# Blocked attention and a gated FFN on one core: 17 units written out in single steps, pair sums folded together, narrow weight loads placed behind short products

## The chip, the cores and the metric

The kernel runs on one core of a Trainium2 chip. Five engines take part: TensorE (PE, with its weight loads shown apart as PEld), VectorE (DVE), ScalarE (ACT), GpSimd (POOL) and SyncE (SP), which issues the transfers. The metric is the device time of one execution in microseconds. Three runs of the kernel before took 1071.14 to 1071.73 us, median 1071.46.

## The reference

Eight batches and eight heads of attention over 576 tokens with 64 features. The mask is by blocks of 64 tokens: a query sees its own block and all before it. The heads are joined to 512 features, and 4608 tokens go through an FFN of 2048 with silu.

```python
scores = scale * np.matmul(q, k.transpose(0, 1, 3, 2))
scores = np.where(block_i >= block_j, scores, -1000000000.0)
scores = scores - np.max(scores, axis=-1, keepdims=True)
attn = np.exp(scores)
attn = attn / (np.sum(attn, axis=-1, keepdims=True) + 1e-09)
x = np.matmul(attn, v)                       # then [8*576, 512]
h = x @ w_in
out = (h * (1.0 / (1.0 + np.exp(-h)))) @ w_out
```

q, k and v are float32. The FFN weights come as float64.

## The kernel before

**Precision.** A float32 operand is split in two parts that TensorE takes at its fast rate: a high part (a cast on ScalarE) and a low part (a subtraction on GpSimd or VectorE). A product is the sum of high by high, high by low and low by high. The weights' float64 is taken apart by words: ScalarE rebiases (`rebias`, L155), VectorE puts the bits together in three operations (`bits`, L159), then come `hi` and `lo`. There are 32 such pieces of weights, w0 to w31; each has a staging buffer that it shares with later work.

**The attention of the first 128 tokens of each batch** is done apart: groups a and b (block 0, class `First`, L427) and c0 to c3 (block 1, class `Second`, L486). They give the first four token blocks of the FFN.

**Units.** The 448 later queries of one batch and head are a unit (class `Unit`, L209), u0 to u63. Keys stand on partitions. The scores come in five segments (`SEG`, L38) of 448, 320, 192, 448 and 64 columns, in three PSUM banks; each segment is two products (`scores`, L242), with q's high and low part. VectorE takes the maximum (`max`, `max2`), subtracts it (`sub`), ScalarE takes the exponential and casts the high part (`exp`, `p_hi`), GpSimd makes the low part (`p_lo`). Nine products with the values (`pv`, L326) sum into bank U: the weights are 128 columns, the values' high part in one half and their low part in the other, and the moving operand is p's high part (ph) or low part (pl). VectorE adds p over the keys (`sums`, then `sums2`, L312, which folds 32-row strips by `quad_fold`, L196, for each unit); `lower` and `fold` join the halves of U, and once two units (a pair) are done `finish` normalizes and splits them into FFN input.

**FFN.** 18 blocks of 256 tokens, 8 steps each. A step has two chunks of 12 products of 256 columns (`ffn1`, L541), a silu on ScalarE, a split of g, and two chunks of 6 products of 512 columns (`ffn2`, L566): 576 chunks in all. In the text a chunk is one `ffn`.

**Order.** The schedule is by hand: every engine takes its instructions in the order in which they are recorded. The table `ORDER` (L47) writes out the weights, the early groups and the first units, up to 72 chunks; a chunk is the word `ffn`, silu and split are `silu` and `part`. From unit 2 on a loop (L661) records each unit the same way, with its predecessors' later stages between, and with `pace` chunks for each: a count that reaches 152 chunks at unit 17, and 7 a unit after that. When the units are used up, the rest of the FFN follows. Forty small products on zeros (`WARM`) stand at the head of TensorE's queue.

Of the kernel before, what the change touches and what calls it, by code (L numbers as in the profile page):

```python
# [47 lines left out]
a.load w0.load w1.load b.load a.load_v a.scores b.scores w2.load a.max:0 w3.load a.max:1 w0.rebias a.sub:0 a.exp:0 a.sub:1  # L48
w0.bits:0 w1.rebias a.sum:0 w0.bits:1 a.exp:1 w4.load a.sum:1 a.norm:0 w0.bits:2 a.norm:1 a.turn:1 w1.bits:0 w0.hi a.turn:0
w1.bits:1 w0.lo b.max:0 a.back:1 w1.bits:2 a.back:0 b.max:1 b.sub:0 a.pv b.load_v a.hi:0 b.sub:1 w5.load a.hi:1 w1.hi w1.lo  # L50
w2.rebias b.exp:1 w4.rebias a.lo:0 a.lo:1 w2.bits:0 b.sum:1 w5.rebias b.exp:0 ffn w2.bits:1 ffn b.sum:0 w2.bits:2 b.norm:0
w3.rebias b.norm:1 w6.load w3.bits:0 b.turn:0 w3.bits:1 w3.bits:2 silu b.turn:1 w2.hi w4.bits:0 b.back:0 b.back:1 w3.hi b.pv
c0.load w7.load w4.bits:1 w2.lo w3.lo b.hi:0 w4.bits:2 b.lo:0 ffn c0.scores:0 w6.rebias b.hi:1 w5.bits:0 part w4.hi w5.bits:1
w8.load b.lo:1 w5.bits:2 w5.hi c0.max:0 w6.bits:0 ffn silu c0.sub:0 ffn w6.bits:1 w4.lo w9.load w5.lo c0.exp:0 w6.bits:2 c0.sum:0
w10.load ffn w8.rebias w7.rebias c0.norm:0 w7.bits:0 w7.bits:1 ffn w9.rebias c0.turn:0 part c0.back:0 c0.scores:1 c0.load_v
w7.bits:2 w6.hi w8.bits:0 w7.hi c0.max:1 w11.load c0.sub:1 w8.bits:1 w6.lo w10.rebias w8.bits:2 w7.lo c0.exp:1 w12.load c0.sum:1
w8.hi c0.norm:1 silu ffn ffn w9.bits:0 w9.bits:1 w9.bits:2 ffn w10.bits:0 c1.load c0.turn:1 c0.back:1 w11.rebias c0.pv w8.lo w9.hi
w10.bits:1 c0.hi w9.lo w10.bits:2 part w10.hi w12.rebias c0.lo w13.load w11.bits:0 ffn ffn w10.lo w11.bits:1 c1.load_v silu
c1.scores:0 w14.load w11.bits:2 part w13.rebias c1.max:0 c1.sub:0 w12.bits:0 w11.hi w11.lo c1.exp:0 ffn ffn ffn silu w12.bits:1
w15.load w12.bits:2 w16.load c1.sum:0 ffn w14.rebias c1.norm:0 w13.bits:0 w13.bits:1 part w13.bits:2 c1.turn:0 c1.back:0  # L60
w14.bits:0 ffn c1.scores:1 c2.load c1.max:1 w12.hi w12.lo w13.hi w13.lo ffn c1.sub:1 w15.rebias c1.exp:1 w17.load silu ffn ffn
w14.bits:1 w14.bits:2 ffn c1.sum:1 c1.norm:1 w15.bits:0 w15.bits:1 w14.hi w14.lo c1.turn:1 c1.back:1 w15.bits:2 w16.rebias part
ffn w15.hi w16.bits:0 c1.pv w17.rebias w16.bits:1 w18.load w16.bits:2 ffn w16.hi c1.hi w19.load w17.bits:0 w15.lo w17.bits:1 ffn
c1.lo c2.scores:0 w18.rebias w17.bits:2 w16.lo c2.max:0 w17.hi c2.sub:0 w18.bits:0 w17.lo silu w20.load w19.rebias ffn ffn
c2.load_v w18.bits:1 ffn w21.load w18.bits:2 ffn part c2.exp:0 w18.hi c2.sum:0 w22.load c2.norm:0 w20.rebias w19.bits:0 w21.rebias
w19.bits:1 w19.bits:2 c2.turn:0 w23.load w20.bits:0 c2.back:0 silu ffn c2.scores:1 c2.max:1 w18.lo part c2.sub:1 w19.hi ffn ffn
w20.bits:1 c2.exp:1 w19.lo ffn ffn silu w20.bits:2 part c2.sum:1 w22.rebias c2.norm:1 w21.bits:0 c2.turn:1 ffn c2.back:1
w21.bits:1 w20.hi w21.bits:2 c3.load w21.hi w20.lo w24.load c2.pv w22.bits:0 w21.lo w25.load w22.bits:1 ffn w22.bits:2 w23.rebias
ffn c2.hi w24.rebias w23.bits:0 w23.bits:1 c2.lo c3.scores:0 w26.load w23.bits:2 c3.max:0 w25.rebias silu w27.load w22.hi part
w23.hi ffn w22.lo w24.bits:0 w23.lo w24.bits:1 ffn c3.sub:0 w24.bits:2 silu ffn c3.load_v w25.bits:0 w25.bits:1 w25.bits:2  # L70
w28.load c3.exp:0 w25.hi w24.hi c3.sum:0 w24.lo w29.load c3.norm:0 ffn ffn w25.lo w26.rebias w26.bits:0 w26.bits:1 part ffn
c3.turn:0 ffn c3.back:0 w26.bits:2 c3.scores:1 ffn c3.max:1 w27.rebias c3.sub:1 c3.exp:1 silu w27.bits:0 c3.sum:1 w26.hi
w29.rebias c3.norm:1 ffn w27.bits:1 w27.bits:2 ffn w28.rebias w26.lo w30.load ffn c3.turn:1 w31.load part c3.back:1 w27.hi
w28.bits:0 w28.bits:1 w28.bits:2 ffn w28.hi w29.bits:0 c3.pv silu w27.lo w28.lo c3.hi w29.bits:1 w29.bits:2 w30.rebias ffn c3.lo
w29.hi ffn w30.bits:0 w29.lo w30.bits:1 w30.bits:2 part w31.rebias ffn silu w30.hi ffn w31.bits:0 ffn part ffn w30.lo w31.bits:1
# [663 lines left out]
```

## Time and profile before

| | |
|---|---|
| median of three runs | 1071.46 us |
| the profiled execution | 1069.56 us, span 1067.8 us |
| TensorE products, busy | 1043.6 us (98%) |
| weight loads, busy | 937.4 us (88%) |
| VectorE, busy | 794.1 us (74%) |
| ScalarE, busy | 765.0 us (72%) |
| GpSimd, busy | 744.4 us (70%) |
| mean granted clock of TensorE | 0.992 |

The shares are means over the whole span. VectorE does nothing once the units are done, so its share while they run is higher than 74%; and a busy TensorE says that a product was under way, not that columns went through at full rate. Unit 0's scores start at 136.18 us, unit 17's at 326.57 us, and the last product ends at 1064.4 us.

### The profile page before, as it was taken

What the parts mean: (1) busy time and instruction counts of PE and PEld (TensorE: products, weight loads), DVE (VectorE), ACT (ScalarE), POOL (GpSimd) and SP (SyncE); (2) the same over time, 40 slices, a digit from 0 to 9 for tenths busy, and PEclk for the clock granted to TensorE, in tenths of its full rate; (3) what the DMA queues carried; (4) which work ended last, traced back from release to release, by engine and by line L of the source; (5) the groups of instructions that cost most, each with busy time, mean ns of one, the idle gap of its engine ahead of it and who ended that gap; (6) DMA issues with size and microseconds to landing.
All of it is one profiled execution on the core that took longest, in us unless ns stands there. A gap on an engine that the chain in (4) does not pass through costs nothing.

```text
span 1067.8 us, 20105 instructions
## 1 busy us (share of the span) xinstructions
PE 1043.6 (98%) x7040; PEld 937.4 (88%) x7040; DVE 794.1 (74%) x2417; ACT 765.0 (72%) x1218; POOL 744.4 (70%) x716
## 2 busy tenths in 40 slices
PE   6899999999999999999999999999999999999998
PEld 6788888888989999989999999999999998999897
DVE  6988569999999888887888888888888888800000
ACT  4787568898887878777877787878787878632222
POOL 1554668888899787777878787878787878632121
PEclk7999999999999999999999999999999999999999
DMA  7666342242322222322222222222322222000000
GB/s 257 220 221 197 82 104 60 53 98 52 76 76 53 72 68 57 78 65 60 71 55 62 63 53 72 53 72 61 83 54 76 55 55 69 8 20 20 1 20 21
DMA packets 35045, 79.95 MB, mean 75 GB/s; under 512 B 4736, under 2 KB 12928, under 8 KB 34944
## 3 DMA queue, kind: packets, MB, share of 16 engines
q1 hardware_dynamic: 34944, 78.66, 26.7%
q8 instruction: 56, 0.92, 0.4%
q14 instruction: 45, 0.37, 0.1%
HBM read 69.21 MB, written 9.44 MB: 74 GB/s over the span
## 4 chain that ended last, share of the span: by engine, by line
PE 77%; DVE 16%; ACT 4%; issue 2%; POOL 1%; DMA 0%; SPq 0%; DVEq 0%; POOLq 0%; ACTq 0%
PE o L576 31%; PE h L551 31%; PE U L331 6%; PE S L253 6%; DVE Mx L190 2%; DVE Dx L190 2%; DVE Xm L200 1%; DVE m L267 1%; DVE T L284 1%; DVE mb L194 1%; DVE Xd L200 1%; DVE S L165 1%; DVE xu L342 1%; DVE S L169 1%; DVE wm L173 1%
## 5 line engine op out<-in xcount | busy, mean ns | idle before, releaser
L551 PE MATMUL h<-x,wi 128*128 128x256 f32 x3456 | 445.4, 282 | 1.4 <-ACT x L480 1.2
L551 PEld LDWEIGHTS h<-x,wi 128*128 128x128 f32 x3456 | 428.7, 189 | 13.0 <-ACT x L480 1.4
L576 PE MATMUL o<-wo,g 128*128 128x512 f32 x1680 | 427.2, 399 | 4.0 <-ACT ot L583 4.0
L576 PEld LDWEIGHTS o<-wo,g 128*128 128x128 f32 x1680 | 302.5, 188 | 68.0 <-ACT ot L583 6.4
L304 POOL TENSOR_TENSOR pl<-p,ph 128x448 fp32r<-128x448 f32 (+1 forms) x192 | 225.4, 1202 | 106.1 <-ACT ph L297 106.1
L564 POOL TENSOR_TENSOR g<-g,g 128x512 fp32r<-128x512 f32 x144 | 186.2, 1293 | 127.7 <-ACT g L563 118.9
L190 DVE TRANSPOSE_TENSOR_REDUCE Mx<-S 64x4 f32<-64x128 f32 (+4 forms) x384 | 129.7, 400 | 97.0 <-PE S L253 96.9
L558 ACT ACTIVATE g<-h 128x512 f32<-128x512 f32 x144 | 86.1, 598 | 102.9 <-POOL g L564 54.1
L190 DVE TRANSPOSE_TENSOR_REDUCE Dx<-p 128x14 f32<-128x448 f32 (+3 forms) x320 | 123.3, 447 | 0.3 <-ACT p L292 0.3
L563 ACT CAST g<-g 128x512 fp32r<-128x512 f32 x144 | 89.4, 621 | 47.1 <-PE o L576 44.9
L230 POOL TENSOR_TENSOR qh<-qkraw,qh 64x576 fp32r<-64x576 f32 x64 | 101.1, 1579 | 11.0 <-ACT qh L226 6.2
L292 ACT ACTIVATE p<-T 128x512 f32<-128x512 f32 (+1 forms) x192 | 103.7, 603 | 0.7
L297 ACT CAST ph<-p 128x512 fp32r<-128x512 f32 (+1 forms) x192 | 101.9, 594 | 0.0
L331 PE MATMUL U<-ph,vc 128*128 128x448 f32 (+3 forms) x320 | 93.0, 303 | 1.5 <-ACT g L558 0.9
L253 PE MATMUL S<-qh 128*128 128x448 f32 (+3 forms) x320 | 93.0, 303 | 0.2
L558 ACT ACT_TABLE_LOAD x71 | 91.1, 1283 | 1.3
L292 ACT ACT_TABLE_LOAD x64 | 82.1, 1283 | 4.2 <-DVE T L282 3.1
L253 PE MATMUL S<-ql,qh 128*128 128x448 f32 (+3 forms) x320 | 83.9, 306 | 0.7 <-POOL ql L232 0.7
L331 PE MATMUL U<-pl,vc 128*128 128x448 f32 (+2 forms) x256 | 79.0, 331 | 1.0 <-POOL pl L304 0.8
L232 POOL TENSOR_TENSOR ql<-qkraw,qh 128x448 fp32r<-128x448 f32 x64 | 74.4, 1162 | 5.0
L226 ACT CAST qh<-qkraw 128x1024 fp32r<-128x1024 f32 x64 | 67.0, 1047 | 9.8 <-DMA qkraw<-in_qk_dram 9.6
L284 DVE TENSOR_TENSOR T<-S,mb 128x256 f32<-128x256 f32 (+2 forms) x192 | 73.1, 407 | 0.0
(101 smaller groups left out, 1162.8 us busy)
## 6 DMA issues: line engine op xcount, KB each, us to landing
qkraw<-in_qk_dram SPq DMA_DIRECT2D x128, 256.0 KB, 4.0
vraw<-in_v_dram SPq DMA_DIRECT2D x64, 160.0 KB, 2.7
wst<-in_moe_w_out_dram SPq DMA_DIRECT2D x15, 512.0 KB, 4.1
out_dram<-ot SPq DMA_DIRECT2D x24, 256.0 KB, 2.0
wst<-in_moe_w_in_dram SPq DMA_DIRECT2D x10, 512.0 KB, 4.4
v<-in_v_dram SPq DMA_DIRECT2D x12, 256.0 KB, 4.7
qk<-in_qk_dram SPq DMA_DIRECT2D x8, 384.0 KB, 4.5
T<-in_moe_w_in_dram SPq DMA_DIRECT2D x6, 512.0 KB, 4.2
```

The lines of the kernel that those rows point to most:

```text
L190: nc.vector.tensor_reduce(out=out, in_=in_, axis=AX.X, op=op, apply_transpose=True)
L230: nc.gpsimd.tensor_tensor(out=u.qh[64:, NQ:], in0=u.raw[64:, NQ:], in1=u.qh[64:, NQ:], op=ALU.subtract)
L253: nc.tensor.matmul(u.ps(c, w, m), u.kk[:, j * P : j * P + m], qq[:, q0 : q0 + w], start=i == 0, stop=i == 1)
L292: nc.scalar.activation(u.p[:, c:e], T[:, c:e], AF.Exp, scale=SCALE)
L297: nc.scalar.copy(u.ph[:, c:e], u.p[:, c:e])
L304: nc.gpsimd.tensor_tensor(out=u.pl[:, c:e], in0=u.p[:, c:e], in1=u.ph[:, c:e], op=ALU.subtract)
L331: nc.tensor.matmul(U[:, q0 : q0 + w], u.vc[:, j, :], pp[:, c : c + w], start=n == 0, stop=n == 8)
L551: nc.tensor.matmul(h[:, f, :], wi[wt][:, c, w], x[:, xt, :], start=n == 0, stop=n == 3 * CT - 1)
L558: nc.scalar.activation(g, hs.pop((blk, d)), AF.Silu)
L563: nc.scalar.copy(g2[:, 0], g)
L564: nc.gpsimd.tensor_tensor(out=g2[:, 1], in0=g, in1=g2[:, 0], op=ALU.subtract)
L576: nc.tensor.matmul(o, g2[:, gt, f, tk], wo[wt][:, 2 * d + f, :], start=d == 0 and n == 0, stop=d == NSTEP - 1 and n == 5,)
```

## The change

- `ORDER` now holds the work of units 0 to 16 as well, all in single steps: exponential, high part and low part by bank (`u4.exp:1`), the two halves of the values' split, the split of g as `g_hi` and `g_lo`, the output's copy and its store. It has 1040 words where it had 496 and ends at 152 chunks; the loop starts at unit 17.
- The units' products come in another order (`QK`, `PV`). The values' high part always stands in the first 64 weight columns, and a product with p's low part loads those 64 columns alone.
- The sums of a pair are folded together: the even unit writes the first half of a wider Dx, the odd one the second, and `sums2` runs once a pair. The 1e-9 is a constant in Xd and no longer an addition.
- An early group takes one exponential and one sum over 1024 columns; for c0 to c3 GpSimd multiplies by the reciprocal. c3 has buffers of its own.
- In the loop, output copies that fall behind the second half of a unit go to VectorE. The warming products are 18.

The places at which the order of the instructions changes are shown as they stand in the built programs. First TensorE in the loop, the value products of one unit, before (U is the bank, ph and pl are p's parts, the last figure is the moving columns, the one before it the weight columns):

```order
L331 MATMUL U<-ph,vc 128x448
L331 MATMUL U<-pl,vc 128x448
L331 MATMUL U<-ph,vc 128x320
L331 MATMUL U<-pl,vc 128x320
L331 MATMUL U<-ph,vc 128x192
L331 MATMUL U<-pl,vc 128x192
L331 MATMUL U<-ph,vc 128x448
L331 MATMUL U<-pl,vc 128x448
L331 MATMUL U<-ph,vc 128x64
```

and the same place after:

```order
L370 MATMUL U<-ph,vc 128x448
L370 MATMUL U<-ph,vc 128x320
L370 MATMUL U<-ph,vc 128x192
L370 MATMUL U<-pl,vc 64x192
L370 MATMUL U<-pl,vc 64x320
L370 MATMUL U<-pl,vc 64x448
L370 MATMUL U<-ph,vc 128x64
L370 MATMUL U<-pl,vc 64x448
L370 MATMUL U<-ph,vc 128x448
```

The 64 columns no longer stand last, and the wide products come before the narrow ones. Next VectorE in the loop, from the end of one unit's subtraction to the next unit's maximum, before (every unit; for an odd one an add, a reciprocal and a transpose follow):

```order
L277 TENSOR_TENSOR T<-S_3895,mb 64x2x64
L200 TENSOR_REDUCE Xd<-Dx 32x14 x4
L320 TENSOR_REDUCE rs<-Xd 32x14 x2
L190 TENSOR_REDUCE Mx<-S_4057 128x14
L190 TENSOR_REDUCE Mx<-S_4058 128x8
```

and after, for an odd unit (for an even one the maximum follows the subtraction at once):

```order
L314 TENSOR_TENSOR T<-S_5223,MR 64x2x64
L242 TENSOR_REDUCE Xd<-Dx 32x28 x4
L359 TENSOR_REDUCE rs<-Xd 32x14 x4
L361 RECIPROCAL rr<-rs 128x14
L237 STREAM_TRANSPOSE MR<-rr 128x448
L233 TENSOR_REDUCE Mx<-S_5385 128x14
```

Four reduces of double width stand for eight. Last ScalarE at the program's start, before (wm is a rebiased weight, S and U are a's scores, p its probabilities):

```order
L157 ACTIVATE wm<-wst 128x512
L395 ACTIVATE S_147<-S_147 128x512
L157 ACTIVATE wm<-wst 128x512
L395 ACTIVATE U_148<-U_148 128x512
L181 CAST wi_73<-wm 128x2x256
L414 COPY p_149<-U_148 128x512
```

and after (MR and wm are rebiased weights, p is a's and T is b's scores):

```order
L200 ACTIVATE wm<-wst 128x512 x2
L224 CAST wi_73<-wm 128x2x256
L439 ACTIVATE p_132<-p_132 128x1024
L200 ACTIVATE MR<-wst 128x512
L439 ACTIVATE T<-T 128x1024
L200 ACTIVATE MR<-wst 128x512
L460 COPY p_132<-U_131 128x512
```

Two rebiases and a cast now stand ahead of a's exponential, which is one instruction.

The diff, cut to its core:

```diff
-WARM = 40
+WARM = 18
 AHEAD = 152
+TABLE = 17
+QK = [0, 1, 3, 2, 4]
+PV = [(0, 0, 128), (1, 0, 128), (2, 0, 128), (2, 1, 64), (1, 1, 64), (0, 1, 64), (4, 0, 128), (3, 1, 64), (3, 0, 128)]
...
-u0.lower u1.p_hi ffn silu u2.load_v u0.sums2 ffn u1.p_lo part
+u2.p_hi:0 u3.sub u4.split_lo u1.lower ffn u1.fold silu ffn u1.sums2 g_hi u2.p_lo:0 u5.load u2.p_hi:1 u4.scores u2.v_hi g_lo
...
-        def split_v(u):
+        def v_hi(u):
             vc = u.vc = sp.tile([P, 5, P], F32R, tag="vc", name="vc")
...
+            nc.scalar.copy(vc[:, :, :64], u.v3)
+        def v_lo(u):
+            nc.gpsimd.tensor_tensor(out=u.vc[:, :, 64:], in0=u.v3, in1=u.vc[:, :, :64], op=ALU.subtract)
...
-            for j, c, q0, w in SEG:
+            for j, c, q0, w in (SEG[i] for i in QK):
...
         def sums(u):
+            n = u.h % 2 * NQB
             for j, c, q0, w in SEG:
-                ttr(Dx[:, q0 // 32 : q0 // 32 + w // 32, j], blocks32(u.p[:, c : c + w]), ALU.add)
+                ttr(Dx[:, n + q0 // 32 : n + q0 // 32 + w // 32, j], blocks32(u.p[:, c : c + w]), ALU.add)
 
         def sums2(u):
-            X = quad_fold(Dx, ALU.add, "Xd")
...
+            quad_fold(Xd, Dx, ALU.add)
+            rs = sp.tile([P, NQB], F32, tag="rs", name="rs")
+            for a in range(4):
+                n = a // 2 * NQB
+                nc.vector.tensor_reduce(out=rs[32 * a : 32 * a + 32], in_=Xd[:, n : n + NQB, :], axis=AX.X, op=ALU.add)
+            rr = sp.tile([P, NQB], F32, tag="rr", name="rr")
+            nc.vector.reciprocal(out=rr, in_=rs)
...
         def pv(u):
...
+            for n, (i, pp, m) in enumerate(PV):
+                j, c, q0, w = SEG[i]
+                nc.tensor.matmul(U[:m, q0 : q0 + w], u.vc[:, j, :m], (u.ph, u.pl)[pp][:, c : c + w], start=n == 0, stop=n == 8)
...
-        def exp(u, k):
-            nc.scalar.activation(u.ps[k], u.ps[k], AF.Exp, scale=SCALE)
...
+        def exp(u):
+            nc.scalar.activation(u.p, u.p, AF.Exp, scale=SCALE)
...
+        def norm(u):
+            u.engine.tensor_tensor(out=u.heads(u.p), in0=u.heads(u.p), in1=u.spread(u.rr), op=ALU.mult)
...
+    def output(blk, d, t):
+        ot = sp.tile([P, DM], F32, tag="ot", name="ot", bufs=2)
+        (nc.vector.tensor_copy if late else nc.scalar.copy)(ot, outs[blk][t])
+        outs[blk][t] = ot
...
-    for i in range(2, n + 2):
+    for i in range(TABLE, n + 2):
...
-        pace = 7 if i >= 17 else (AHEAD - count[0]) // (17 - i)
+        pace = 6 + (count[0] <= AHEAD + 7 * (i - TABLE))
...
-        if w:
+        if w and w.h % 2:
             w.sums2()
+        late.append(u)
         ffn(3)
+        late.pop()
```

## Rows read from the trace of the kernel before

**Rows 1.** Stretches of the span: length, busy us of each engine with instructions, TensorE's clock, DMA.

```profile
55.15:136.18 81.03, 80.53 (x634) 70.55 (x633) 60.37 (x99) 58.29 (x91) 45.15 (x36) 1.00 0.52 156
136.18:326.57 190.39, 184.37 (x1143) 161.94 (x1142) 176.99 (x579) 159.46 (x251) 160.28 (x159) 1.00 0.31 74
326.57:929.00 602.43, 601.01 (x3857) 547.11 (x3856) 507.49 (x1647) 476.47 (x760) 484.06 (x470) 1.00 0.24 62
```

**Rows 2.** Timeline of TensorE in the loop: start, us, engine, line, product, count.

```profile
601.68 1.56 PE L576 MATMUL o<-wo,g 128*128 128x512 f32 x6
603.08 0.36 PE L331 MATMUL U<-ph,vc 128*128 128x448 f32 x1
...
603.78 0.25 PE L331 MATMUL U<-ph,vc 128*128 128x192 f32 x1
603.87 0.27 PE L331 MATMUL U<-pl,vc 128*128 128x192 f32 x1
603.98 0.39 PE L331 MATMUL U<-ph,vc 128*128 128x448 f32 x1
604.21 0.36 PE L331 MATMUL U<-pl,vc 128*128 128x448 f32 x1
604.41 0.19 PE L331 MATMUL U<-ph,vc 128*128 128x64 f32 x1
604.44 1.64 PE L576 MATMUL o<-wo,g 128*128 128x512 f32 x6
...
608.74 0.37 PE L253 MATMUL S<-qh 128*128 128x448 f32 x1
...
610.10 0.22 PE L253 MATMUL S<-ql,qh 128*64 128x64 f32 x1
610.16 3.05 PE L576 MATMUL o<-wo,g 128*128 128x512 f32 x12
```

**Rows 3.** Groups of instructions, score weight loads: busy us, mean ns, idle before.

```profile
L253 PEld LDWEIGHTS S<-qh 128*128 128x128 f32 x256 | 48.3, 189 | 5.0 <-PE S L253 1.4 <-POOL x L362 0.4 <-POOL qh L230 0.3
...
L253 PEld LDWEIGHTS S<-qh 128*64 128x64 f32 x64 | 8.6, 134 | 1.0
```

**Rows 4.** Busy time of the score products alone, units 17 to 56.

```profile
326.57:837.50 510.93, 62.99 (x400) 59.73 (x399) 1.00 0.25 64
```

**Rows 5.** Groups of instructions, VectorE's small reduces.

```profile
L200 DVE TENSOR_REDUCE Xd<-Dx 32x14 f32<-32x70 f32 x256 | 54.4, 213 | 2.6
L267 DVE TENSOR_REDUCE m<-Xm 32x14 f32<-32x56 f32 x256 | 51.6, 201 | 4.8
...
L320 DVE TENSOR_REDUCE rs<-Xd 32x14 f32<-32x56 f32 x128 | 25.8, 202 | 3.0
...
L204 DVE TENSOR_SCALAR rs<-rs 128x14 f32<-128x14 f32 x32 | 12.8, 401 | 1.1
```

**Rows 6.** Timeline of the start, TensorE and VectorE.

```profile
12.91 1.13 PE L461 MATMUL o<-qk 64*64 64x64 f32 x32 [2.13 <-DMA qk<-in_qk_dram]
...
22.07 0.58 PE L551 MATMUL h<-x,wi 128*128 128x256 f32 x1 [1.18 <-ACT x L480]
...
26.95 1.28 DVE L405 TENSOR_TENSOR T<-o,rr 128x512 f32<-128x512 f32 x2
...
40.71 0.63 PE L411 MATMUL S<-ident,p 128*128 128x128 f32 x4 [0.73 <-DVE p L405]
...
49.36 1.15 PE L528 MATMUL S<-p,v 128*64 128x64 f32 x32 [0.72 <-ACT p L414]
...
54.13 1.09 PE L514 MATMUL S<-qk 64*64 64x128 f32 x16
```

**Rows 7.** Groups: a cast of 1024 columns, and GpSimd's low part of 512.

```profile
L564 POOL TENSOR_TENSOR g<-g,g 128x512 fp32r<-128x512 f32 x144 | 186.2, 1293 | 127.7 <-ACT g L563 118.9 <-DVE S L169 4.3 <-POOL wi L184 0.8
...
L226 ACT CAST qh<-qkraw 128x1024 fp32r<-128x1024 f32 x64 | 67.0, 1047 | 9.8 <-DMA qkraw<-in_qk_dram 9.6
```

**Rows 8.** Stretch at the start, with TensorE's granted clock.

```profile
11.39:28.46 17.07, 11.00 (x129) 9.70 (x130) 15.39 (x32) 9.06 (x16) 2.55 (x2) 0.50 0.57 201
```

More of the change, by code (lines that the diff above doesn't have):

```diff
@@ L47 @@
 ORDER = """
[L48 to L75, printed above, removed]
@@ new lines @@
+ffn c1.exp w30.rebias ffn c1.sum g_hi w29.rebias g_lo ffn w28.bits:2 w29.bits:0 c1.norm ffn w29.bits:1 w29.bits:2 silu ffn
+w30.bits:0 w29.hi w27.lo w30.bits:1 c1.turn:0 w30.bits:2 ffn c1.back:0 c3.load w30.hi c1.turn:1 c2.load ffn c1.back:1 w31.rebias
+c1.pv w28.hi w31.bits:0 g_hi w28.lo ffn w31.bits:1 c1.hi c2.load_v w31.bits:2 g_lo c1.lo ffn silu c3.scores:0 w31.hi g_hi ffn
+c3.max:0 g_lo c3.sub:0 c2.scores:0 w29.lo silu ffn c2.max:0 w30.lo c2.sub:0 c3.scores:1 ffn c3.max:1 c3.sub:1 c2.scores:1 ffn
@@ new lines @@
+u0.p_hi:0 store u0.exp:2 u0.p_lo:0 ffn u1.load_v u2.split_hi u1.max2 ffn u0.p_hi:1 u2.split_lo output ffn u1.sub silu ffn
+u0.p_hi:2 u0.p_lo:1 output u0.sums u3.load g_hi u2.scores u0.p_lo:2 ffn g_lo u2.max u1.exp:0 u0.pv u1.exp:1 u3.split_hi u2.max2
+ffn u1.exp:2 u3.split_lo u0.lower ffn u1.p_hi:0 u1.p_hi:1 u2.sub u1.v_hi ffn u1.v_lo u0.fold silu u3.scores u1.p_lo:0 u1.sums
+u2.load_v g_hi u4.load u1.p_hi:2 u1.p_lo:1 ffn u3.max u1.p_lo:2 ffn u2.exp:0 g_lo u3.max2 u2.exp:1 u1.pv u2.exp:2 u4.split_hi ffn
@@ new lines @@
+u11.p_hi:1 u11.p_lo:0 u11.v_hi u10.fold ffn u11.p_hi:2 u12.sub u11.p_lo:1 ffn u11.v_lo u11.sums2 u12.exp:0 u11.p_lo:2 u13.scores
+u12.load_v u12.exp:1 g_lo ffn u12.exp:2 u14.split_hi u13.max u11.pv u14.split_lo ffn u13.max2 silu u11.lower g_hi ffn u12.v_hi
+g_lo u12.p_hi:0 u11.fold u11.mult ffn output u12.v_lo u13.sub silu u12.p_lo:0 u12.p_hi:1 ffn u13.load_v u12.p_hi:2 u15.load
+u12.p_lo:1 g_hi u12.sums u11.x_hi u14.scores store u12.p_lo:2 output ffn u14.max g_lo u12.pv u13.exp:0 u11.x_lo u15.split_hi
@@ L413, in back @@
         def back(u, k):
-            nc.scalar.copy(u.p[k], u.ps[k])
+            nc.scalar.copy(u.part(k), u.ps[k])
         def tiles(u, blk, n):
@@ L684, in attn_ffn @@
         if u:
-            u.split_v()
+            u.v_hi()
+            u.v_lo()
             if i + 1 < n:
```

283 lines of the change are left out of this document (165 added, 118 removed).

## The prediction

> **What bounds the kernel now.** I read the stretches first, then TensorE's own order of time, then the start. In the stretches [rows 1] the reader is to see that one engine is never far from full: TensorE is busy 601.01 of 602.43 us from unit 17's scores on, so there its time alone counts; from 136.18 to 326.57 us (units 0 to 16) TensorE has 184.37 of 190.39 and VectorE 176.99, so two engines are nearly full and neither quite. A busy TensorE is not one that streams, so the second view is its timeline [rows 2]. A product of 448 columns is followed by the next start 200 ns later (604.21 to 604.41), one of 192 after 90 ns (603.78 to 603.87), one of 64 after 30 ns: 0.45 ns a column. But the product behind the second 192 starts 110 ns later, and the next one 230 ns later where 200 is due; and the six products behind the 64 columns take 1.64 us where six take 1.56. Each product needs its own weight load, and a load lies beside the product before it. A load of 128 columns thus needs about 110 ns, and where the product in front is shorter, the rest shows: 20 to 25 ns behind 192 columns, 80 ns behind 64. The third view is the start, which comes below.
>
> **Order of the products (QK, PV).** Before, one unit's value products show 20 behind the second segment's first product, 30 behind its second and 80 behind the last one: 130 ns. The score products go through the same widths and show the same 50, then 30 where a 64-column product with a 64-column load follows another (60 from 610.10 to 610.16, against the 30 of 604.41 to 604.44), and 80 at the end: 160 ns. A 64-column load therefore takes about 60 ns, and its row has 134 ns against 189 for the wide one, 55 less, as the steps have 50 less [rows 3]. After, the value products put the narrow loads behind 192, 192 and 320 columns (nothing shows), the 128-column load of the 64-column product behind 448 (nothing), one narrow load behind the 64 (30 ns), and a 448-column product last (nothing): 30 instead of 130. The score products lose one of the two exposures beside the 192s: 135 instead of 160. That is 0.125 us a unit. From unit 17 on TensorE sets the pace: forty units take 510.93 us, 12.77 each [rows 4], of which scores are 1.42 (608.74 to 610.16) and value products 1.36 (603.08 to 604.44) [rows 2]. 47 units x 0.125 = **5.9 us** that nothing else can take back: VectorE is busy 507.49 of 602.43 there [rows 1]. The bounds are 1.2 (only the score order, 47 x 0.025, if narrow loads were no shorter) and 8 (64 units).
>
> The Trainium skill ("TensorE: Matmul & The Clock Gate", Weight-path perf modes) has a rule that speaks against this edit: a fast weight load is switched on when the number of weights is 128 and the type isn't FP32, so a 64-column load would lose it. The same page (LDWEIGHTS) makes a load's time proportional to its columns, 107 ns for 128 by its formula; by that the term stays at 5.9, by the other it drops to 1.2. The steps of 60 and 110 ns agree with the second.
>
> **Folding the sums of a pair together, 17 units in the table.** Before, a pair costs VectorE eight reduces of 213 ns, four of 202 and an add of 401 [rows 5]: 2.91 us; the reciprocal and the broadcast stay. After, it is four reduces twice as wide and four of 202. The wide reduce isn't in the trace; from 56 to 70 elements a reduce rises from 201 to 213, so 140 elements give about 280 ns, bounded by 213 (width costs nothing) and 426 (all of it). 4 x 0.28 + 0.81 = 1.93, so 0.98 us a pair, 0.5 a unit (bounds 0.2 and 0.63). In the stretch of units 0 to 16 that takes VectorE from 177.0 to 168.6. TensorE's floor there: 92 chunks (60 are issued before unit 0's scores and 152 before unit 17's, in the table of either kernel). A chunk is (12.77 - 1.42 - 1.36 - 0.16 for products between)/7 = 1.405, and 17 units at 2.78 less 0.125 are 45.1, with 17 x 0.16 = 2.7: 129.3 + 47.8 = 177. If VectorE keeps its present 93% of the stretch, the stretch is 181.3; neither engine can be packed fully, so I take 182 where 190.4 stood: **8.4 us**. One bound is the floor (13.4). The other is no gain at all but the loads' 17 x 0.125 = 2.1; a finer order can also wait worse, and as far as the present 6 us of TensorE's idling would double, it is 4 us slower. I choose between them by VectorE's row, since that is the fuller of the two by work after a wait. From unit 17 on this fold is worth nothing: VectorE waits for TensorE there.
>
> **The start.** The order puts w0 first and w1 behind all of a and b; ScalarE's queue has w1's rebias ahead of a's exponential. Before, the sixth large load was b's second, and the products that waited for it start at 12.91 [rows 6]; the same place now has w1, so the rebias ends at about 13.6, the cast of w0 at 14.2, and a's exponential starts then. VectorE, which holds w1's bits ahead of a's sum, goes on at 13.6: from there to a's last low part stand thirteen operations of 512 columns at 0.64 (two take 1.28 [rows 6]), four of 1024 at an estimated 1.15 (bounds 0.64 and 1.28, and the cast of that width has 1.05 [rows 7]) and two pairs of small ones, under 0.4 each: 13.7 us. The first FFN product starts at about 27.5 where it stood at 22.07. By then b is normalized and w2 done, which came later before. TensorE's granted clock was 0.50 from 11.39 to 28.46 [rows 8], 1.2 GHz, to 6.4 us past the first FFN product; I let the same 6.4 us cost 3.2 again. Twelve chunks at 1.405, two score groups of 1.09 and the 3.2 put the end of chunk 11 at 49.8; what the old kernel had also done at 55.15 (the end of c1's first scores at 54.13 plus their 1.02: c0's transposes and value products and those scores) is 3.5 more (two transposes of 0.63, 1.15 and 1.09): 53.3. From 55.15 to 136.18 TensorE is busy 80.53 of 81.03 [rows 1], so a lead is kept and a lag isn't made up. Gain **1.8 us**; bounds +5 (the clock is already up) and -5 (the 5.4 us by which the first product is late, nothing of it made up). Forty warming products become 18: free, since the clock had fallen before the first FFN product anyway.
>
> **Edits at nothing.** One exponential a group and normalizing on GpSimd: 4 x 2.6 us, by two of its 512-column operations [rows 7] (bounds 1.3 and 5.2), beside FFN products, and GpSimd is busy 45.15 of 81.03 there; without that cover it would be 10 us. VectorE's output copies (nine) stand where it waits 15% of the time; splitting hi and lo into single tokens adds no instruction. The DMAs stay 296; in the table a store stands some words behind its copy, so that the loads behind it in SP's queue wait no longer than before, when it came right after the copy.
>
> **Sum.** The profiled execution took 1069.56 us (span 1067.8, 1.76 around it), 1.9 below the median 1071.46. 1069.56 - 5.9 - 8.4 - 1.8 = 1053.5, on the median's scale 1055.4; I take **1056**, as the middle of the stretch is optimistic by up to a microsecond.
>
> **Rivals.**
> 1. Narrow loads cost as much as wide ones: for it, no row has a narrow load beside a long product; against it, the steps of 60 and 110. The loop's 5.9 becomes 1.2: 1061. Chance 0.07.
> 2. The stretch of 17 units doesn't shrink: VectorE's saved time becomes waiting, as each unit still passes scores, maximum, exponential, low part and value products through single buffers. For it: VectorE idles 13.4 us there already. Only 2.1 of the 8.4 stay: 1062. Chance 0.15.
> 3. The stretch reaches TensorE's floor and the start gains its 5: 1056 - 5 - 3 = 1048. For it: VectorE's new 168.6 leaves 8 us of room; against it, none of the engines was ever packed so at the start. Chance 0.15.
> 4. Slower: the clock stays at half, since the first chunks come as VectorE hands out weights and not in one run. Each chunk at half costs 1.405 more; the 3.2 hold two of them, and the gain of 15.5 is gone after 11 more. With 20 chunks at half it is 1056 + 18 x 1.405 = 1081. Against it: the clock rose 6.4 us after the first FFN product although TensorE waited for input around it [rows 6], and w9, the last weights that chunk 10 wants, are 22 VectorE operations behind the first product: 27.5 + 14 + 2 for cast and low part is 43.5, and chunk 10 comes at 46.9. Chance 0.06. The Trainium skill (same page, The HAM clock gate) says that the throttled state is the default and activity lifts it; by that fewer warming products are a risk only if TensorE idles behind them.
>
> **Numbers.** The forecast has 0.57. A change under 0.2% (2.1 us) can't be told from none here; 1069 to 1074 takes the far tails of rivals 2 and 4 and of the start's bound, 0.04; above it 0.05; faster 0.91. The range from 1047 to 1067 leaves out rival 4, part of 3 and the tails.
>
> **What would show it.** Right: the value products' nine starts without a step over 205 ns but the 60 behind the 64; units 12.64 us apart from unit 17 on; units 0 to 16 in 180 to 185 us with VectorE near 168; the first FFN product at 27 to 28 and the clock up by 35. Wrong: narrow loads that still part the products by 110 ns, VectorE under 90% in that stretch with TensorE waiting for scores to be freed, or half clock past 40 us.

## The result, and the profile after

The changed kernel takes 1061.5 us in the median of four runs (1060.57 to 1061.71) against 1071.38: a ratio of 0.991, 95% interval 0.990 to 0.992. It is 9.9 us faster; the forecast had 15.4. The profiled execution took 1061.71 us, its span is 1060.0. Marked by the first score product of a unit, the span of before and after parts like this (us):

| part | before | after | change | forecast |
|---|---|---|---|---|
| up to unit 0's scores | 136.18 | 133.51 | -2.7 | -1.8 |
| units 0 to 16 | 190.39 | 186.24 | -4.2 | -8.4 |
| unit 17 to unit 63 | 589.87 | 587.72 | -2.2 | -5.9 |
| unit 63 to the end | 151.39 | 152.54 | +1.1 | 0 |

The table compares two single executions. The one of the kernel before took 1069.56 us, 1.8 below its median, so its parts add to 7.9 us and not to 9.9.

The first view is the busy time by stretches (length, TensorE, its weight loads, VectorE, ScalarE, GpSimd, then the granted clock); it answers to [rows 1, 8].

```profile
8.18:25.25 17.07, 8.93 (x176) 7.47 (x172) 15.64 (x25) 7.45 (x12) 3.05 (x2) 0.50 0.72 256
25.25:60.55 35.30, 32.26 (x289) 28.70 (x289) 32.33 (x50) 27.84 (x45) 22.43 (x18) 1.00 0.77 229
...
133.51:319.75 186.24, 181.29 (x1143) 160.80 (x1142) 175.42 (x539) 155.67 (x250) 161.62 (x160) 1.00 0.27 72
319.75:920.16 600.41, 597.75 (x3858) 544.18 (x3857) 514.11 (x1533) 469.20 (x748) 482.63 (x471) 1.00 0.24 63
```

VectorE (the third busy time) is at 175.42 us in units 0 to 16, not near 168. Behind unit 17 TensorE's gaps have grown, from 1.42 us to 2.66. TensorE's timeline answers to [rows 2]: two groups of scores, and the value products between them.

```profile
396.96 0.25 PE L289 MATMUL S<-qh 128*128 128x192 f32 x1
397.05 0.28 PE L289 MATMUL S<-ql,qh 128*128 128x192 f32 x1
397.16 0.19 PE L289 MATMUL S<-qh 128*64 128x64 f32 x1
397.19 0.22 PE L289 MATMUL S<-ql,qh 128*64 128x64 f32 x1
...
402.98 0.60 PE L370 MATMUL U<-ph,vc 128*128 128x448 f32 x3
403.42 0.60 PE L370 MATMUL U<-pl,vc 128*64 128x192 f32 x3
403.85 0.19 PE L370 MATMUL U<-ph,vc 128*128 128x64 f32 x1
403.88 0.40 PE L370 MATMUL U<-pl,vc 128*64 128x448 f32 x1
404.12 0.37 PE L370 MATMUL U<-ph,vc 128*128 128x448 f32 x1
405.09 1.66 PE L629 MATMUL o<-wo,g 128*128 128x512 f32 x6 [0.61 <-ACT ot L637]
407.48 1.68 PE L629 MATMUL o<-wo,g 128*128 128x512 f32 x6 [0.72 <-ACT ot L637]
...
410.42 0.37 PE L289 MATMUL S<-qh 128*128 128x448 f32 x1
...
411.82 0.36 PE L599 MATMUL h<-x,wi 128*128 128x256 f32 x1
```

The reader is to see two things. The value products run as forecast: three products of 448, 320 and 192 columns start within 0.44 us, the three behind them within 0.43, and only one step is long: the 448 columns behind the 64 take 240 ns (403.88 to 404.12) where 200 are usual, which is where the forecast's 30 ns show. The median unit fell from 12.776 to 12.690 us. And TensorE now waits twice for an output copy (counted up to the product after it, 0.88 and 0.99 us beyond the usual steps), and again at 813.41 and 815.80; before, it waited only twice between units 17 and 63 (472.42 and 882.33, 0.97 and 0.98):

```profile
472.42 0.50 PE L576 MATMUL o<-wo,g 128*128 128x512 f32 x1 [0.71 <-ACT ot L583]
```

46 units at 0.086 us less are 4.0 us; the stalls, 1.8 us longer in all, take nearly half of that back, and 2.2 are left. What stands ahead of that copy is read on VectorE, GpSimd and ScalarE. VectorE:

```profile
396.45 0.65 DVE L233 TRANSPOSE_TENSOR_REDUCE Mx<-S 128x14 f32<-128x448 f32 x1 [0.68 <-PE S L289]
397.36 1.50 DVE L233 TRANSPOSE_TENSOR_REDUCE Mx<-S 128x8 f32<-128x256 f32 x5 [0.26 <-PE S L289]
...
401.94 1.83 DVE L384 TENSOR_TENSOR xu<-xu,MR 128x448 f32<-128x448 f32 x1
```

GpSimd:

```profile
400.49 1.30 POOL L617 TENSOR_TENSOR g<-g,g 128x512 fp32r<-128x512 f32 x1
401.86 1.43 POOL L265 TENSOR_TENSOR qh<-qkraw,qh 64x576 fp32r<-64x576 f32 x1
```

ScalarE:

```profile
403.81 0.75 ACT L401 CAST x<-xu 128x128 fp32r<-128x128 f32 x3 [4.87 <-DVE xu L384]
404.46 0.57 ACT L637 COPY ot<-o 128x512 f32<-128x512 f32 x1
```

The closing multiplication of a pair (L384) begins 0.08 us behind a GpSimd subtraction (401.86 to 403.29), takes 1.83 us and ends 0.48 behind that subtraction's end. Wherever in this trace the multiplication is lengthened, it ends 0.48 to 0.51 us behind the GpSimd operation that ran when it began. ScalarE's cast of the pair waits for it, and the output copy is queued behind the cast. In the kernel before, the same pair of operations stood the other way round, by 0.17 us (VectorE, then GpSimd):

```profile
609.35 2.03 DVE L190 TRANSPOSE_TENSOR_REDUCE Mx<-S 128x14 f32<-128x448 f32 x6 [1.71 <-PE S L253]
...
614.46 0.58 DVE L346 TENSOR_TENSOR xu<-xu,rb 128x448 f32<-128x448 f32 x1
```

```profile
614.63 1.71 POOL L230 TENSOR_TENSOR qh<-qkraw,qh 64x576 fp32r<-64x576 f32 x1
```

There the multiplication took 0.58 and GpSimd's operation 1.71 instead of 1.43: whichever starts second waits. Over the whole trace the multiplication went from 659 to 1276 ns, while VectorE's operations of this size with one operand in PSUM did not change (in the kernel before, the pair's sum took 603 ns and the subtraction 606; they are L381 and L319 here). After:

```profile
L384 DVE TENSOR_TENSOR xu<-xu,MR 128x448 f32<-128x448 f32 x32 | 40.8, 1276 | 0.1
...
L319 DVE TENSOR_TENSOR T<-S,MR 128x448 f32<-128x448 f32 x64 | 38.9, 607 | 1.5
L381 DVE TENSOR_TENSOR xu<-U,t 64x448 f32<-64x448 f32 x64 | 38.7, 605 | 5.5 <-ACT t L375 4.1 <-issue 0.4
L242 DVE TENSOR_REDUCE Xd<-Dx 32x28 f32<-32x140 f32 x128 | 36.4, 284 | 1.3
```

The Trainium skill (SBUF — State Buffer, Who interferes with whom) states this: a VectorE instruction with two SBUF inputs contends with a GpSimd instruction that reads SBUF, and of the two one blocks the other for a whole instruction. The rows above agree: the held multiplication ends 0.48 us behind GpSimd's operation, and the held GpSimd operation takes 1.71 us for 1.43.

The theory to test: the new score order (QK) puts the last products of the middle PSUM bank behind the 448 columns of the next bank, so that VectorE's second maximum waits (0.26 us at 397.36, and "x5" behind a gap where before stood one run of six); the multiplication comes 0.3 us later and loses to GpSimd; the copies behind it stall TensorE. The rival: the loss belongs to the new order of the table or to ScalarE's queue, and the score order is as good as forecast.

The 1.1 us lost behind unit 63 are one more wait. Here TensorE waits for a silu, which stands in ScalarE's queue behind the cast of the last pair but one; that pair's multiplication took 1.34 us:

```profile
925.47 0.97 PE L599 MATMUL h<-x,wi 128*128 128x256 f32 x6 [0.93 <-ACT g L606]
```

The kernel before has no such wait, nor has any run below in which the changed kernel's score order is undone or its multiplication comes early.

### The profile page after: what moved, and what is told of

Read it like the earlier page. It is cut to its first block, busy times and chain, and to the rows that moved or that the text cites. A ratio compares the mean times of both kernels' runs of the same rounds, so it can differ in the third digit from the quotient of the medians.

```text
span 1060.0 us, 19884 instructions
## 1 busy us (share of the span) xinstructions
PE 1033.0 (97%) x6996; PEld 930.3 (88%) x6996; DVE 792.0 (75%) x2238; ACT 746.3 (70%) x1193; POOL 750.6 (71%) x721
## 4 chain that ended last, share of the span: by engine, by line
PE 77%; DVE 11%; POOL 4%; ACT 3%; DMA 3%; issue 2%; SPq 0%; DVEq 0%; POOLq 0%; ACTq 0%
PE h L599 31%; PE o L629 30%; PE S L289 7%; PE U L370 7%; DVE Mx L233 1%; DMA qkraw<-in_qk_dram 1%; DVE wm L216 1%; DVE S L212 1%; POOL pl L344 1%; DVE S L208 1%; DVE Dx L233 1%; DVE xu L384 1%; DMA wst<-in_moe_w_in_dram 1%; POOL ql L267 1%; POOL qh L265 1%
## 5 line engine op out<-in xcount | busy, mean ns | idle before, releaser
L599 PE MATMUL h<-x,wi 128*128 128x256 f32 x3456 | 440.5, 282 | 0.9 <-ACT g L606 0.9
L599 PEld LDWEIGHTS h<-x,wi 128*128 128x128 f32 x3456 | 429.0, 189 | 13.4 <-ACT g L606 2.7
L629 PEld LDWEIGHTS o<-wo,g 128*128 128x128 f32 x1680 | 305.9, 188 | 66.7 <-ACT ot L637 4.3
L617 POOL TENSOR_TENSOR g<-g,g 128x512 fp32r<-128x512 f32 x144 | 186.2, 1293 | 127.9 <-ACT g L612 121.2
L233 DVE TRANSPOSE_TENSOR_REDUCE Mx<-S 64x4 f32<-64x128 f32 (+4 forms) x384 | 135.5, 404 | 76.6 <-PE S L289 76.1
L265 POOL TENSOR_TENSOR qh<-qkraw,qh 64x576 fp32r<-64x576 f32 x64 | 95.2, 1488 | 17.9 <-ACT qh L261 10.9
L336 ACT CAST ph<-p 128x512 fp32r<-128x512 f32 (+1 forms) x192 | 104.2, 595 | 0.4 <-PE U L370 0.3
L289 PE MATMUL S<-qh 128*128 128x448 f32 (+3 forms) x320 | 92.6, 302 | 2.2 <-DVE T L319 1.0
L606 ACT ACT_TABLE_LOAD x66 | 84.7, 1283 | 1.2
L330 ACT ACT_TABLE_LOAD x62 | 79.5, 1283 | 6.5 <-DVE Dx L233 5.3
L267 POOL TENSOR_TENSOR ql<-qkraw,qh 128x448 fp32r<-128x448 f32 x64 | 76.9, 1202 | 8.5 <-PE S L575 3.5
L401 ACT CAST x<-xu 128x256 fp32r<-128x256 f32 (+3 forms) x80 | 22.6, 339 | 81.7 <-DVE xu L384 81.7
L370 PE MATMUL U<-ph,vc 128*128 128x448 f32 (+3 forms) x320 | 74.6, 298 | 2.2 <-POOL vc L276 2.2
L321 DVE TENSOR_TENSOR T<-S,MR 128x256 f32<-128x256 f32 (+2 forms) x192 | 73.2, 408 | 0.0
```

What stands on the lines that cost most here:

```text
L233: nc.vector.tensor_reduce(out=out, in_=in_, axis=AX.X, op=op, apply_transpose=True)
L265: nc.gpsimd.tensor_tensor(out=u.qh[64:, NQ:], in0=u.raw[64:, NQ:], in1=u.qh[64:, NQ:], op=ALU.subtract)
L289: nc.tensor.matmul(u.ps(c, w, m), u.kk[:, j * P : j * P + m], qq[:, q0 : q0 + w], start=i == 0, stop=i == 1)
L336: nc.scalar.copy(u.ph[:, c:e], u.p[:, c:e])
L370: nc.tensor.matmul(U[:m, q0 : q0 + w], u.vc[:, j, :m], (u.ph, u.pl)[pp][:, c : c + w], start=n == 0, stop=n == 8)
L599: nc.tensor.matmul(h[:, f, :], wi[wt][:, c, w], x[:, xt, :], start=n == 0, stop=n == 3 * CT - 1)
```

## The experiments

All times are medians of four or five runs, with the ratio to the kernel before in the same job. The part of the span from unit 17 to 63 and the multiplication's mean from unit 17 on are from the profiled execution; stalls are TensorE's waits before output copies in that part, counted as above.

| kernel | us | ratio, 95% | 17 to 63 | mult. ns | stalls us |
|---|---|---|---|---|---|
| before | 1071.4 | | 589.87 | 625 | 1.95 |
| changed | 1061.5 | 0.990 to 0.992 | 587.72 | 1303 | 3.73 |
| changed, old score order | 1055.8 | 0.985 to 0.988 | 584.17 | 839 | 0.86 |
| changed, multiplication early | 1055.4 | 0.984 to 0.987 | 583.22 | 872 | 0 |
| changed, GpSimd reordered | 1057.7 | 0.985 to 0.989 | 586.35 | 674 | 3.11 |
| changed, wide loads | 1063.4 | 0.992 to 0.995 | 590.07 | 1283 | 1.96 |
| before, new score order | 1075.8 | 1.003 to 1.006 | 593.56 | 1208 | 6.36 |
| before, new value loads | 1065.4 | 0.994 to 0.996 | 584.90 | 775 | 3.79 |

**The score order undone** in the changed kernel:

```
-QK = [0, 1, 3, 2, 4]
+QK = [0, 1, 2, 3, 4]
```

> The changed kernel with one line undone: the score products run by segments 0, 1, 2, 3, 4 again. Theory A: in the new order the last product of the middle PSUM bank (segment 2) comes one 448-column pair later, so VectorE's maximum of segment 1 waits about 0.26 us a unit for it (12.1 us over the trace), while TensorE saves only 7 ns a unit. Undone, that wait is gone, the multiplication that closes a pair starts ahead of GpSimd's subtraction again (mean near 0.6 instead of 1.28 us), two of the four stalls before output copies (0.9 us each) go, and the stretch of units 0 to 16 loses 1 to 3 us: 1057 to 1060 us, against 1061.5. Rival B (the forecast's term): the order is worth 25 ns a unit and nothing hangs on the bank: 1063.

Measured 1055.79 us: 5.7 faster than the changed kernel (5.0 by the ratios), more than theory A asked. The maxima run as one group again, with no wait inside, and the part from unit 17 on is TensorE's own time (length, TensorE second):

```profile
133.51:318.05 184.54, 180.37 (x1144) 160.66 (x1142) 173.23 (x539) 155.47 (x250) 162.12 (x160) 1.00 0.28 73
318.05:902.22 584.17, 583.85 (x3780) 531.34 (x3778) 486.99 (x1504) 462.99 (x736) 474.30 (x462) 1.00 0.25 65
```

Its median unit is 12.685 us against 12.690, and units without a stall differ by 5 ns in the mean, so on TensorE the order was worth next to nothing. Of the gain in the profiled executions 3.6 us lie between units 17 and 63 (2.9 of them stalls) and 1.0 behind unit 63, where the wait for the silu is gone. 1.7 lie in units 0 to 16, but that share is not certain: the three runs with this table and the old order took 184.53, 185.23 and 186.13 us there (the last with 3.4 us at half clock), five with the new order 185.35 to 186.34.

**The score order alone**, put into the kernel before (the same line, the other way):

> The kernel before with another part of the change alone: the score products in the order 0, 1, 3, 2, 4. The forecast gave it 25 ns a unit, 1.6 us faster in all: 1069.8. Theory A now: TensorE gains at most 7 ns a unit, the maximum of segment 1 waits 0.26 us a unit for the last product of its bank, and the multiplication, which started less than 0.2 us ahead of GpSimd's subtraction, is now held behind it (0.62 becomes 1.2 to 1.4 us from unit 17 on), so that the stalls before the output copies double: 3 to 6 us slower, 1074.5 to 1077.5. Rival B: the order only does this together with the table: within 1 us of 1071.4.

Measured 1075.84, 4.8 slower, as theory A says; rival B falls. The median unit went from 12.776 to 12.766; the wait inside the maxima is there, and the multiplication is held (VectorE, then GpSimd):

```profile
487.29 1.50 DVE L191 TRANSPOSE_TENSOR_REDUCE Mx<-S 128x8 f32<-128x256 f32 x5 [0.25 <-PE S L254]
...
491.87 1.58 DVE L347 TENSOR_TENSOR xu<-xu,rb 128x448 f32<-128x448 f32 x1
```

```profile
491.55 1.43 POOL L231 TENSOR_TENSOR qh<-qkraw,qh 64x576 fp32r<-64x576 f32 x1
```

So no table is needed for the loss; this one line brings it.

**GpSimd's order alone.** The next unit's low parts behind the pair's:

```
         units[i + 1].split_hi()
-        units[i + 1].split_lo(); load of unit i + 2
 if z and z.h % 2: z.mult(); z.x_hi(); z.x_lo()
+        units[i + 1].split_lo(); load of unit i + 2
```

> The changed kernel with only GpSimd's own order altered from unit 17 on: the two low parts of the next unit's q and k stand behind the pair's low part instead of ahead of it, so GpSimd waits for the pair while VectorE multiplies. VectorE's, ScalarE's and TensorE's orders stay. Theory A (a VectorE operation with two SBUF operands is held to the end of a GpSimd instruction that is running): the multiplications that meet that low part of q and k (1.63 to 1.84 us each, about half of them) take 0.58, the mean from unit 17 on falls from 1.30 to 0.7 to 0.9 us, the four stalls of TensorE before the copies (3.7 us in all) shrink to at most 1.5, and the run is 2 to 3.5 us shorter: 1058 to 1059.5 us. Rival B: the length is the multiplication's own or VectorE's, and GpSimd only happens to run beside it: the mean stays near 1.3 and the time at 1061.5, or up to 1063 as the low parts come later.

Measured 1057.68. With nothing changed on VectorE, the multiplication has its 0.58 us back wherever GpSimd waits (VectorE, then GpSimd):

```profile
731.88 0.58 DVE L384 TENSOR_TENSOR xu<-xu,MR 128x448 f32<-128x448 f32 x1
```

```profile
732.81 1.47 POOL L405 TENSOR_TENSOR x<-xu,x 128x64 fp32r<-128x64 f32 x3 [1.29 <-ACT x L401]
734.36 1.43 POOL L265 TENSOR_TENSOR qh<-qkraw,qh 64x576 fp32r<-64x576 f32 x1
```

This isolates GpSimd as what held it. The 3.8 us are less clear. Between the profiled executions, 3.2 us apart, 1.4 lie between units 17 and 63 and 0.8 behind unit 63; the other 1.1 lie ahead of unit 17, where this edit changes nothing. The point on the stalls fell: they shrank only to 3.1 us, because just at the two places before output copies another GpSimd operation (L617) holds it (1.38 us at 400.81, 1.67 at 807.94).

**The multiplication early.** From unit 17 on:

```
 z.fold()
+if z.h % 2: z.mult()
 u.max2()
...
-z.mult()
 z.x_hi(); z.x_lo()
```

> The changed kernel with the pair's closing multiplication moved, from unit 17 on, from behind the folding of the maximum to right behind the pair's sum on VectorE, where GpSimd has nothing to run. Theory A: the multiplication (two SBUF operands) is held while a GpSimd instruction runs, and what hangs on it, ScalarE's cast of the pair and the output copy queued behind that, makes the four stalls of TensorE (0.88, 0.99, 0.88, 0.99 us): its mean falls from 1.28 to about 0.8 us over the trace and to 0.58 from unit 17 on, the four stalls go, 1057.5 to 1058.5 us. Rival B: the stalls come from ScalarE's own order, and the maximum's folding, 0.6 us later now, delays the subtraction and with it the next scores: 1061.5 to 1064.

Measured 1055.43, all four stalls gone. But the means did not fall to 0.58: at the new place it often meets another GpSimd subtraction (0.75 or 0.97 us). What counts is that it ends sooner, so that ScalarE's cast waits 18.1 us in all for it from unit 17 to 63, not 70.3 (changed kernel first):

```profile
ACT x L401 <- DVE xu L384: 70.3, 23, 4.9
...
PEld o L629 <- ACT ot L637: 4.3, 4, 1.2
```

```profile
ACT x L401 <- DVE xu L384: 18.1, 12, 1.6
```

**Wide loads**, order kept:

```
-PV = [... (2, 1, 64), (1, 1, 64), (0, 1, 64), (4, 0, 128), (3, 1, 64) ...]
+PV = [... (2, 1, 128), (1, 1, 128), (0, 1, 128), (4, 0, 128), (3, 1, 128) ...]
```

> The changed kernel with every weight load of the value products 128 columns wide, order kept (so the low products also add low times low). Theory A (the forecast's steps): 25 ns show again behind each of the two 192s and 80 instead of 30 behind the 64, some 100 ns a unit, 47 units: 4.7 us, 1066 us in all. Rival B: the order alone had done it, the width is worth nothing: 1061.5 to 1062.

Measured 1063.43: 1.9 slower (2.7 by the ratios), between the two. The steps are as theory A has them, two groups longer by 60 and 40 ns:

```profile
403.59 0.65 PE L370 MATMUL U<-pl,vc 128*128 128x192 f32 x3
404.08 0.19 PE L370 MATMUL U<-ph,vc 128*128 128x64 f32 x1
404.11 0.45 PE L370 MATMUL U<-pl,vc 128*128 128x448 f32 x1
404.39 0.36 PE L370 MATMUL U<-ph,vc 128*128 128x448 f32 x1
```

The median unit grew by 0.10 us to 12.79, 46 times 4.6; but two of the four stalls vanished (1.8 us), and unit 63 to the end and the start were 0.8 us shorter together.

**The value loads alone** in the kernel before:

```
+PV = [(0, 0, 128), (1, 0, 128), (2, 0, 128), (2, 1, 64), (1, 1, 64), (0, 1, 64), (4, 0, 128), (3, 1, 64), (3, 0, 128)]
...
-hi, lo = vc[:, :, u.a : u.a + 64], vc[:, :, 64 - u.a : 128 - u.a]
+hi, lo = vc[:, :, :64], vc[:, :, 64:]
...
```

> The kernel before with one part of the change alone: the value products' new order and narrow loads (high part of v always in the first 64 columns). Nothing else moves, and the multiplication of a pair still starts ahead of GpSimd's subtraction. Theory A (the forecast's steps): 100 ns a unit from unit 17 on, 4.7 us, and little before that, as VectorE is fuller there: 1066 to 1067 us against 1071.4. Rival B: the time comes back as another wait, as it did in the whole change: under 2.5 us.

Measured 1065.43, 5.6 faster: theory A, slightly low. From unit 17 to 63 the profiled execution is 5.0 us shorter, although the stalls grew here too (3.8 us for 1.95); ahead of unit 17 it is 2.3 us longer, which was not traced. The median unit, 12.679, hides that the units go by fours here (12.56, 12.68, 12.68, 12.61): their mean without stalls is 12.63, so 0.14 less than before.

**The fold undone**, in the changed kernel:

```
-quad_fold(Xd, Dx, ALU.add)
+for n in (0, NQB):
+    quad_fold(Xd[:, n : n + NQB], Dx[:, n : n + NQB], ALU.add)
```

> The changed kernel with the pair's eight partial sums folded by eight reduces of 70 elements a partition instead of four of 140, at the same place in the order: 8 x 0.213 against 4 x 0.284, 0.57 us of VectorE a pair. Theory A: VectorE sets the pace of units 0 to 16, so that stretch grows by 3 to 4.8 us (8.5 pairs) and nothing changes behind it: 1064.5 to 1066 us. Rival B: the stretch is set by waits between the engines, and VectorE's time is worth little there: 1061.5 to 1062.5.

Measured 1063.98 (0.993 to 0.995), 2.5 slower (3.1 by the ratios), between the theories: units 0 to 16 took 187.83 us (1.6 more) for 3.2 us more of VectorE, nothing from unit 17 to 63 (587.98).

**The table's multiplications left out:**

```
-if method:
+if method == "mult":
+    pass
+elif method:
```

> The changed kernel without the closing multiplications of the pairs that the table orders (8 pairs; their outputs stay unnormalized): 8.3 us of VectorE leave the stretch of units 0 to 16, 2.8 of them being the time for which GpSimd holds the multiplications. Theory A: VectorE's time sets that stretch, at the price that the fold showed (3.2 us of VectorE for 1.6 of the stretch) or fully: the stretch is 4 to 8 us shorter, 1053.5 to 1057.5. Rival B: the waits between the engines set it: less than 1.5 us, 1060 or more.

Measured 1055.67 us, with these seven pairs left unnormalized. Units 0 to 16 take 181.11 us, 5.1 less, and VectorE (the third busy time) is busy for 92.6% of them:

```profile
133.10:314.21 181.11, 177.81 (x1143) 160.94 (x1142) 167.62 (x532) 156.52 (x251) 160.00 (x161) 1.00 0.29 75
```

Theory A. This is the point of the forecast, 168.6 in 181.3, reached by taking out as much VectorE time as the forecast had thought gone.

**Warming products:**

```
-WARM = 18
+WARM = 40
```

> The changed kernel with 40 warming products at the start, as before, instead of 18. Theory A (the forecast): they are worth nothing, since the granted clock has fallen to half before the early attention either way and rises with its work: 1061.5 us, within 1. Rival B: more warming keeps the clock up in the early attention, whose products then take half the time: 1 to 3 us faster. Rival C: the products stand ahead of the first scores in TensorE's queue and delay them: 0.5 to 2 us slower.

Measured 1061.91 (0.990 to 0.993): nothing, as the forecast had it, though the clock itself differed: in the profiled execution it fell at 14.37 and was back at full at 31.44 us, where the changed kernel has 8.18 and 25.25. In both it fell behind the first scores (7.25 and 6.19), not ahead of the early attention as theory A had it.

**Together.** The old score order (QK as above) and the early multiplication (the two edits of `z.mult()` above):

> The changed kernel with the old score order and the early multiplication from unit 17 on together. Theory A: from unit 17 on either of them alone has already taken all of TensorE's waiting away (584.2 and 583.2 us from unit 17 to unit 63, where TensorE is busy for all but 0.3), so the two do not add up there; what the score order alone gives in units 0 to 16 and at the end is kept: 1053.5 to 1055 us. Rival B: the gains of 5.7 and 6.1 us are of different origin and add up: 1050.

Measured 1054.74 (0.983 to 0.986), the lowest median, though not told apart from either edit alone: from unit 17 to 63 it takes 583.31. No stall is left, yet the multiplication takes 1.20 us in the mean from unit 17 on: held or not, it costs TensorE nothing where it ends early enough for the cast and the copy behind it. With GpSimd's order (the edit of `split_lo()` above) in place of the early multiplication:

> The changed kernel with the old score order and with GpSimd's order altered from unit 17 on (the next unit's low parts behind the pair's), the multiplication where it was. Theory A: the two remove the same loss from unit 17 on (TensorE waiting for output copies behind the held multiplication), so that part ends at TensorE's 583 to 584 us and does not go below; the stretch before keeps the order's gain: 1054 to 1056 us. Rival B: the gains, 5.7 and 3.8 us alone, add: 1052.

Measured 1056.61 (0.986 to 0.989): no sum of gains either, and a little above theory A, as two stalls (1.7 us) are left and the part from unit 17 to 63 takes 585.02. And the first pair of edits with the table's seven multiplications moved behind their sums, as here for unit 3:

```
-u3.fold u4.p_hi:1 ffn ... u4.v_lo ffn u3.mult u4.p_lo:1
+u3.fold u3.mult u4.p_hi:1 ffn ... u4.v_lo ffn u4.p_lo:1
```

> The old score order and the early multiplication from unit 17 on, and in the table, too, each pair's closing multiplication stands right behind the pair's sum and its folded reciprocal (7 pairs). Theory A: VectorE's time sets units 0 to 16 at about 0.6 us a us (5.1 us of the stretch for 8.3 us of multiplications left out), and the place in VectorE's order decides whether GpSimd holds the multiplication: if the mean falls from 1.01 to 0.7 us or less, 2 us of VectorE go and 1.2 of the stretch, 1053.5 us against 1054.7. Rival B: GpSimd is busy 87% of that stretch, so another place is as often taken: mean near 1.0, 1054.7 within 0.7. Rival C: the earlier multiplication delays the maxima and with them the next scores: slower, 1056.

Measured 1055.63 (0.985 to 0.988), not told apart from the pair of edits alone and just above rival B's range; theory A falls. The mean in the table is 1.08 us against 1.01, so the new places meet GpSimd as often as the old.

## Why the forecast was right in direction and 5.5 us short

- **Value loads: right.** About 0.1 us a unit was forecast for them; the experiments show 0.10 (wide loads, by the median unit) and 0.14 (value loads alone, by the mean of the units without a stall). Rival 1 falls with the wide loads.
- **Score order: the step that failed.** "The score products lose one of the two exposures beside the 192s: 135 instead of 160" put 25 ns a unit to its credit. On TensorE the order does work that way, but it is worth little: a group of scores is 22 ns shorter by it in the kernel before and 8 in the changed one, a unit without a stall 13 and 5. And it costs 5.7 us in the changed kernel and 4.8 in the old one. The claim that the loop's 5.9 us were such "that nothing else can take back", since VectorE has room there, looked at VectorE's total only. With the score order undone that part is 5.7 us shorter than before. That is the forecast's size, but partly by luck: the products give 4.2 (46 units at 0.091), and 1.1 are stalls of the kernel before, which the forecast did not count.
- **What was not asked:** who stands behind the pair's multiplication, and what GpSimd runs when it starts. It led by 0.17 us before; VectorE's delay of 0.3 us was enough.
- **Units 0 to 16: mis-sized**, 8.4 forecast, 4.2 measured, 4.3 to 5.9 in the three runs with the old score order. The price was right (VectorE at 94.2% of the stretch after, 93.9 and 92.6 in two experiments; 93 forecast). VectorE's own time was wrong: 175.42 instead of 168.6. The wide reduce took 284 ns where 280 was estimated [rows 5], but eight pairs end in that stretch, not 8.5, and the dropped add was cheaper there (342 ns, not the 401 of the whole trace): 6.8 us of reduces and adds went, net of 0.4 that rs took more. Seven multiplications took 2.8 us more. The groups of this stretch before, then after:

```profile
L200 DVE TENSOR_REDUCE Xd<-Dx 32x14 f32<-32x70 f32 x64 | 13.6, 213 | 0.7
...
L320 DVE TENSOR_REDUCE rs<-Xd 32x14 f32<-32x56 f32 x32 | 6.5, 202 | 0.8
L346 DVE TENSOR_TENSOR xu<-xu,rb 128x448 f32<-128x448 f32 x7 | 5.5, 781 | 0.0
...
L204 DVE TENSOR_SCALAR rs<-rs 128x14 f32<-128x14 f32 x8 | 2.7, 342 | 0.3
```

```profile
L242 DVE TENSOR_REDUCE Xd<-Dx 32x28 f32<-32x140 f32 x32 | 9.1, 283 | 0.4
L384 DVE TENSOR_TENSOR xu<-xu,MR 128x448 f32<-128x448 f32 x7 | 8.3, 1179 | 0.1
L359 DVE TENSOR_REDUCE rs<-Xd 32x14 f32<-32x70 f32 x32 | 6.9, 217 | 0.6
```

These 4.0 us of durations are only 1.6 of busy time: records of neighbouring operations overlap, by 23.1 us in all before (579 records that add to 200.1) and by 20.8 after (539 that add to 196.2), and the busy time counts an overlap once. The forecast took off durations as if all of them were time; why less overlaps now was not traced. Rival 2 comes nearer in size (4.2 against its 2.1) but not in mechanism, since VectorE's idle time there did not grow: it fell from 13.4 to 10.8 us. What sets the rest, 9 us above TensorE's forecast floor of 177, stays open.
- **The start: right in sign, and near in size by luck.** The gain is 2.7 for 1.8. The first FFN product started at 26.79 (27.5 forecast), the exponential at 12.97 (14.2). The 3.2 us for the half clock were not paid: here it was back at full at 25.25, ahead of the first FFN product, and not 6.4 us behind it as before [rows 8]. With the 0.7 us by which the first product came early, that would have made the gain 5.7. But the clock did not set it: in six further runs with the same start it came back at 28.91 to 30.33 us, and unit 0's scores started at 132.95 to 134.46 all the same. One of them is the run with the old score order, whose first FFN product came at 27.69:

```profile
9.25:29.73 20.48, 12.05 (x217) 10.67 (x218) 18.83 (x30) 11.58 (x20) 5.43 (x4) 0.50 0.73 260
```

In either run TensorE then stands still for the same thing, GpSimd's normalization of an early group (L450), and ends up at the same place. The changed kernel first, then that run:

```profile
60.55 0.66 PE L457 MATMUL S<-ident,MR 128*128 128x128 f32 x4 [1.49 <-POOL MR L450]
```

```profile
60.59 0.66 PE L457 MATMUL S<-ident,MR 128*128 128x128 f32 x4 [1.09 <-POOL MR L450]
```

The forecast had this normalization under "Edits at nothing", covered by FFN products. It is not quite covered: it takes 1.90 us, less than the 2.6 estimated, but begins late, at 58.60. So one error hid a good part of the other; the rest was not traced, and no run has the normalization earlier.
- Rivals 3 and 4 are out: units 0 to 16 stay 9 us above TensorE's forecast floor, and no stretch of the profiled execution past 25.25 us shows half clock.

## What to carry to other kernels

Before reordering products for TensorE, look up who reads the banks they close: a reader that waits for a whole bank is late when the bank's last product moves back, by whatever TensorE does in between. For each VectorE operation with two SBUF operands, look at what GpSimd runs when it starts and what is queued behind it; a lead of 0.2 us is no margin. Test each part of a change alone: here one line lost 5 of the 15 us that the rest had won. And where two runs of the same code differ early but agree later, look for the wait at which they meet: it shows what set the stretch.
